# Token blocks of up to four units, alternating input places, and a mix in 32-column products

## The chip, the cores and the metric

The kernel runs on one core of one Trainium2 chip. The metric is the device time of one execution in microseconds; several runs are given by their median. A run of this kernel varies by some 0.2%.

## What is computed

Three layers follow each other. The first is a recurrent attention over 768 time steps for 4 x 8 heads of 48 channels; the second and the third are feed-forward layers of 3072 tokens x 384, one with 2048 hidden channels and a sigmoid gelu, the other with 1024 and a softmax-weighted, layer-normalised activation.

```python
def _attn_ref(r, k, v, w, u):
    for t in range(S):
        kt, vt, rt, wt = (k[:, :, t], v[:, :, t], r[:, :, t], w[:, :, t])
        cur = np.einsum('bhd,bhe->bhde', u[None] * kt, vt)
        y[:, :, t] = np.einsum('bhd,bhde->bhe', rt, state + cur)
        state = wt[:, :, :, None] * state + np.einsum('bhd,bhe->bhde', kt, vt)
def _moe_ref(x, w_in, w_out):
    h = x @ w_in
    return (h * (1.0 / (1.0 + np.exp(-1.702 * h)))) @ w_out
def _moe2_ref(x, w_in, w_out, g_ln):
    h = x @ w_in
    e = np.exp(h - np.max(h, axis=-1, keepdims=True))
    solu = h * e / (np.sum(e, axis=-1, keepdims=True) + 1e-09)
    mu = np.mean(solu, axis=-1, keepdims=True)
    var = np.mean((solu - mu) ** 2, axis=-1, keepdims=True)
    return ((solu - mu) / np.sqrt(var + 1e-06) * g_ln) @ w_out
```

The weights come as 64-bit floats; the kernel turns them into 32-bit ones on the chip.

## The kernel before

The 3072 tokens are 24 units of 128. A unit is 128 time steps of one batch entry, all eight heads; six units in a row carry a state. `BLOCKS` (line 28) groups the units for the first feed-forward layer: three blocks of two units and six of three. `LAST` is the last block's number.

**Attention of a unit.** `f_scan`, `f_r1`, `f_r0`, `f_back` and `f_k` (lines 133 to 165) form running products of the decay and scale `r` and `k` by them (VectorE, `f_r1` on GpSimd, a small copy `pc` on ScalarE). `turn_k` and `copy_k` transpose the scaled `k`. `scores` multiplies `k` by `r` within a half of 64 time steps, `masked` keeps the lower triangle and writes it into `R0` and `R1`, beside the scaled `r`. `states` and `update` carry the state. `mix` (line 308) is one product per head and half: `R0` or `R1` is the stationary operand, 64 columns of it, and `vs0` or `vs1`, state and values, the moving operand of 48 columns; the two halves write partitions 0 to 63 and 64 to 127 of one bank. `bonus`, `bonus_sum`, `bonus_mul` and `total` add the term with `u`. `turn` transposes the result; `out_hi` and `out_lo` split it into a high and a low part, `XH` and `XL`, which together keep 32-bit accuracy in products of the faster type. `XH` and `XL` have room for six units, used as a ring (line 383, 345).

**First feed-forward layer.** For a block and each of 16 slices `f` of the hidden channels: `rise` (line 517) makes nine products into a bank `h` (two banks by turns), `gelu` runs twice on ScalarE, `rest` forms the low part on VectorE, `fall` (line 541) makes nine products into three sums `acc`. `fall` runs two steps after `rise` (`drain(2)`). At a block's end `store` copies the sums to `x2a` or `x2b`, where the second layer reads them. A product has as many moving columns as the block has tokens: 256 or 384.

**Order.** Everything is put in order by hand. `START` (line 38) is a list of steps for the opening: attention of units 0 to 8, the conversion of the first layer's weights (`Lw` load, `N0` to `N3`, `H`, `C`), and the blocks 0 to 2. The raw weights pass through three places in `x2b` (`raw1`), the temporaries through six in `x2a` (`temp1`), since both are free then. From block 3 on, `steps_of` (line 654) hangs the attention of the next block's units between the 16 steps of a block, at the steps `ones` and `twos` and the ones behind them: `one`, `scan`, `back`, `two`, `rest_of`. During the last block the weights of the second layer are converted in the same way (`w2_steps`).

**Tail.** For each unit: `head` (line 580, 18 products of 512 columns), `soft` on ScalarE and VectorE, `turn_q` (transposes and split, into the room of `XH` and `XL`), `tail` (24 products of 384 columns), store.

Of the kernel before, what the change touches and what calls it, by code (L numbers as in the profile page):

```python
# [9 lines left out]
U32 = mybir.dt.uint32  # L10
# [16 lines left out]

BLOCKS = [(0, 2), (2, 2), (4, 2)] + [(u, 3) for u in range(6, NU, 3)]
LAST = len(BLOCKS) - 1

PASSED = (0, 1, 2, 4, 5, 6, 8, 9, 10, 12, 13, 15, 16, 17, 17, 17)
# [39 lines left out]
class Attention:  # L71
# [236 lines left out]
    def mix(self, i, e=None):  # L308
        mm, s = self.nc.tensor.matmul, self.st[i]
        one = e is None  # L310
        if i < QUADS:
            s["y"] = y = self.bank(i, 1)[:, 0:HD]
            y = [y[:, h * D:(h + 1) * D] for h in range(H)]
        else:

            s["y"] = y = self.bank(i, 3).rearrange("p (b c) -> p b c", b=2)[:, :, 4 * C:4 * C + 4 * D]
            y = [y[:, h // 4, (h % 4) * D:(h % 4 + 1) * D] for h in range(H)]
        if e is not None:
            mm(out=s["y"], lhsT=self.ident, rhs=s["vd"], start=True, stop=False)
        for h in range(H):  # L320
            c, e = slice(h * C, (h + 1) * C), slice(h * D, (h + 1) * D)
            mm(out=y[h][0:64], lhsT=s["R0"][0:112, c], rhs=s["vs0"][0:112, e], start=one, stop=one or h == 7)  # L322
            mm(out=y[h][64:128], lhsT=s["R1"][:, c], rhs=s["vs1"][:, e], start=one, stop=one or h == 7)  # L323

# [18 lines left out]

    def out_hi(self, i, hi):
        s, t = self.st[i], slice((i % 6) * 128, (i % 6) * 128 + 128)
        s["xv"] = s["xT"][:, 0:HD].rearrange("p (c t) -> p c t", c=3)
        self.nc.scalar.activation(out=hi[:, :, t], in_=s["xv"], func=AF.Copy)

    def out_lo(self, i, hi, lo, e=None):
        s = self.st.pop(i)  # L350
        t, x = slice((i % 6) * 128, (i % 6) * 128 + 128), s["xv"]
        if e is None:
# [10 lines left out]
def rwkv_moe_moe2(ctx: ExitStack, tc: tile.TileContext, rkw, nat, vn, v2n, cst, w1, w2i, w2o, gln, out):  # L363
# [10 lines left out]
    x2a = cp.tile([128, 4 * 1152], F32, name="x2a")  # L374
    x2b = cp.tile([128, 4 * 1152], F32, name="x2b")

    x2 = {}
    for b, (u0, n) in enumerate(BLOCKS):
        if b < 2:
            u0, n = 0, 4  # L380
        t = (x2a, x2b)[u0 // 12][:, (u0 % 12) * HD:(u0 % 12 + n) * HD]
        x2[b] = u0, t.rearrange("p (c t) -> p c t", c=3)
    XH, XL = (cp.tile([128, 3, 6 * 128], F32R, name=f"xT{a}") for a in "hl")

# [16 lines left out]
    def gtile(a, name):  # L401
        return cp.tile([128, 384], F32R, tag=a, name=name, bufs=3)

# [17 lines left out]
    def raw1(f):  # L421
        return x2b[:, (f % 3) * 1536:(f % 3 + 1) * 1536].bitcast(U32)

# [5 lines left out]

    order = START.split()  # L430
    def temp1(f):
        return x2a[:, (f % 6) * 768:(f % 6 + 1) * 768]

# [20 lines left out]
    def w2_steps(p):  # L454
# [8 lines left out]
        def load(src, n):  # L463
            raw = p.tile([128, 768], U32, tag="raw", name="raw", bufs=5)[:, 0:2 * n]
            t = p.tile([128, 384], U32, tag="t", name="t", bufs=7)[:, 0:n]
# [47 lines left out]
    def tokens(j):  # L513
        u0, n = BLOCKS[j]
        return n * 128, slice((u0 % 6) * 128, (u0 % 6 + n) * 128)

    def rise(j, f):
        TB, tok = tokens(j)
        h_ps = G[j, f] = single(f"h{j}_{f}")[:, 0:TB]
# [32 lines left out]

    def store(j, outs):
        for e in outs:
            nc.scalar.activation(out=x2[j][1][:, e], in_=acc[e][:, 0:512 if j < 2 else tokens(j)[0]], func=AF.Copy)
# [13 lines left out]

    XS, Q, O, SM, E = {}, {}, {}, {}, {}  # L570

# [49 lines left out]
    def turn_q(i, halves=(0, 1)):  # L621

        o = (i % 2) * 1024
        hi, lo = [t.rearrange("p c t -> p (c t)")[:, o:o + 1024] for t in (XH, XL)]
        for b in halves:
# [8 lines left out]
    def tail(i, part):  # L634
# [11 lines left out]
        o_ps = O.pop(i)  # L646
        ob = gtile("gh", f"ob{i}").bitcast(F32)
        nc.scalar.activation(out=ob, in_=o_ps, func=AF.Copy)
# [5 lines left out]
    def steps_of(j):  # L654
# [4 lines left out]
        u0, n = BLOCKS[j + 1]  # L659
        ones, twos = (1, 6, 11), (4, 9, 14)  # L660
        for i, a, b in zip(range(u0, u0 + n), ones, twos):
# [18 lines left out]

            def back(i=i, nx=nx, nn=nn):
                if nn:
                    at.f_back(i + 2)
                if nx:
                    at.bonus_sum(i + 1)

            def two(i=i, nx=nx):
                at.turn(i)
                if nx:
                    at.states(i + 1)  # L690
                    at.load_v2(i + 2)
                at.out_hi(i, XH)
                at.out_lo(i, XH, XL)
                if nx:
# [5 lines left out]

            def rest_of(i=i):
                at.f_r0(i + 2)
                at.f_k(i + 2)

            S[a] += [one]
            if nn:
                S[a + 1] += [scan]
            S[a + 2] += [back]
            S[b] += [two]
# [9 lines left out]
        D=at.states, DA=lambda i: at.states(i, 0), DB=lambda i: at.states(i, 1), U1=lambda i, e=None: at.update(i, 0, e), U2=lambda i, e=None: at.update(i, 1, e), X=at.mix, V=at.total,  # L719
        T=at.turn, O=lambda i: at.out_hi(i, XH), OL=lambda i, e=None: at.out_lo(i, XH, XL, e),  # L720
        N0=lambda f: conv1(f, 0), N1=lambda f: conv1(f, 1), N2=lambda f: conv1(f, 2), N3=lambda f: conv1(f, 3),
# [156 lines left out]
```

## Time and profile before

| what | value |
|---|---|
| median of 3 runs | 754.5 us (753.58 to 754.74) |
| the profiled execution, its own time | 753.76 us |
| its span, first to last instruction | 750.8 us |
| TensorE products, busy | 732.8 us (98%) |
| TensorE weight loads, busy | 688.8 us |
| VectorE busy | 502.2 us (67%) |
| ScalarE busy | 304.0 us (40%) |
| GpSimd busy | 153.3 us (20%) |
| mean granted TensorE clock | 0.999 of full speed |

Busy times of TensorE come from products that overlap each other in the pipeline, so the sum of their durations is larger than the time that they take in a row. The start-to-start distance of two products is what one costs in a full stream. All rows are of one profiled execution. Names: PE is TensorE, PEld its weight loads, DVE VectorE, ACT ScalarE, POOL GpSimd, SP the queue that issues the transfers.

### The profile page before, as it was taken

The numbers are of one execution on the slowest core, as the hardware profiler recorded it, in microseconds if no ns is written. First come the engines' busy times: TensorE is split into PE (matmuls) and PEld (weight loads), VectorE is DVE, ScalarE is ACT, GpSimd is POOL, SyncE is SP. The second block draws the span as 40 slices with busy tenths as digits, with TensorE's granted clock in tenths as the row PEclk, the third lists the DMA queues.
The fourth block names the chain that finished last, engine by engine and source line by source line (L and its number), as shares of the span: only waits on it lengthen the run. The fifth ranks groups of instructions, "written<-read, shape, count | busy, mean of one in ns | idle before, by whom it ended". The sixth has DMA issues, their size and how long they took to land.

```text
span 750.8 us, 15429 instructions
## 1 busy us (share of the span) xinstructions
PE 732.8 (98%) x6350; PEld 688.8 (92%) x6350; DVE 502.2 (67%) x885; ACT 304.0 (40%) x660; POOL 153.3 (20%) x158
## 2 busy tenths in 40 slices
PE   3899999999999999999999999999999999999998
PEld 2689999999999999999999999999999999999987
DVE  8899999887666665666566552498555555555553
ACT  2465453333223223322322322475544444444443
POOL 5351312541222222222222120040000000000000
PEclk9999999999999999999999999999999999999999
DMA  8965723334222221222222100451000000000000
GB/s 254 237 221 176 243 76 116 97 86 113 75 74 69 73 71 41 74 75 74 66 75 65 32 6 2 134 153 51 1 22 22 21 22 22 22 22 22 31 23 32
DMA packets 26103, 58.02 MB, mean 77 GB/s; under 512 B 3409, under 2 KB 18769, under 8 KB 26033
## 3 DMA queue, kind: packets, MB, share of 16 engines
q1 hardware_dynamic: 26032, 57.04, 25.7%
q8 instruction: 49, 0.80, 0.5%
q14 instruction: 22, 0.17, 0.1%
HBM read 52.31 MB, written 4.72 MB: 76 GB/s over the span
## 4 chain that ended last, share of the span: by engine, by line
PE 96%; DVE 2%; ACT 1%; issue 0%; DMA 0%; ACTq 0%; DVEq 0%
PE acc L548 28%; PE h L523 27%; PE o L641 13%; PE left L588 7%; PE right L588 7%; PE att L322 3%; PE right L628 1%; PE left L628 1%; PE att L215 1%; PE att L238 1%; PE att L338 1%; PE att L263 1%; PE d L446 1%; PE att L231 0%; PE att L275 0%
## 5 line engine op out<-in xcount | busy, mean ns | idle before, releaser
L548 PE MATMUL acc<-gh,w 128*128 128x384 f32 (+1 forms) x864 | 224.0, 323 | 0.0
L523 PE MATMUL h<-xTh,w 128*128 128x384 f32 (+1 forms) x864 | 180.2, 319 | 0.0
L531 ACT ACTIVATE gh<-h 128x384 fp32r<-128x384 f32 (+1 forms) x144 | 65.6, 455 | 266.4 <-PE h L523 257.9
L548 PEld LDWEIGHTS acc<-gh,w 128*128 128x128 f32 x864 | 152.7, 189 | 2.3
L538 DVE TENSOR_TENSOR gl<-h,gh 128x384 fp32r<-128x384 f32 (+1 forms) x144 | 73.4, 511 | 121.4 <-ACT h L533 120.9
L523 PEld LDWEIGHTS h<-xTh,w 128*128 128x128 f32 x864 | 142.9, 189 | 1.0 <-ACT w L448 0.5
L548 PE MATMUL acc<-gl,w 128*128 128x384 f32 (+1 forms) x432 | 137.3, 318 | 0.1
L523 PE MATMUL h<-xTl,w 128*128 128x384 f32 (+1 forms) x432 | 90.6, 318 | 0.0
L548 PEld LDWEIGHTS acc<-gl,w 128*128 128x128 f32 x432 | 81.7, 189 | 0.3 <-DVE gl L538 0.3
L523 PEld LDWEIGHTS h<-xTl,w 128*128 128x128 f32 x432 | 72.0, 189 | 0.0
L142 POOL TENSOR_TENSOR R<-rkw,P 64x512 f32<-64x512 f32 x24 | 30.5, 1272 | 197.2 <-DVE P L136 182.2
L641 PE MATMUL o<-w,xTh 128*128 128x384 f32 x384 | 70.5, 335 | 0.0
L641 PEld LDWEIGHTS o<-w,xTh 128*128 128x128 f32 x384 | 67.0, 188 | 0.2
L533 ACT ACTIVATE h<-h 128x384 f32<-128x384 f32 (+1 forms) x144 | 65.1, 452 | 0.0
L203 POOL TENSOR_TENSOR vd<-vs,dg 64x384 f32<-64x384 f32 x48 | 43.7, 910 | 78.7 <-PE att L338 55.6
L618 POOL TENSOR_TENSOR sm<-sm,mhalf 128x1 f32<-128x1 f32 x24 | 13.2, 548 | 218.5 <-DVE sm L617 218.5
L250 DVE TENSOR_TENSOR R<-att,cc 64x256 f32<-64x256 f32 (+1 forms) x82 | 37.2, 454 | 10.9 <-PE att L323 9.5
L641 PE MATMUL o<-w,xTl 128*128 128x384 f32 x192 | 43.0, 346 | 0.0
L613 ACT ACTIVATE e<-q,sm 128x1024 f32<-128x1024 f32 x24 | 27.6, 1152 | 30.3 <-DVE sm L616 29.8
L588 PE MATMUL right<-w,x2h 128*128 128x512 f32 x144 | 37.1, 392 | 0.0
L588 PE MATMUL left<-w,x2h 128*128 128x512 f32 x144 | 37.0, 392 | 0.0
L179 POOL TENSOR_TENSOR nr<-nr,nk 128x384 f32<-128x384 f32 x24 | 26.0, 1083 | 43.5 <-DMA nk<-in_nat 42.4
(170 smaller groups left out, 1255.6 us busy)
## 6 DMA issues: line engine op xcount, KB each, us to landing
rkw<-in_rkw SPq DMA_DIRECT2D x22, 676.4 KB, 5.3
x2b<-in_w SPq DMA_DIRECT2D x16, 768.0 KB, 5.0
nr<-in_nat SPq DMA_DIRECT2D x24, 192.0 KB, 3.0
nk<-in_nat SPq DMA_DIRECT2D x24, 192.0 KB, 2.6
vs<-in_vn SPq DMA_DIRECT2D x48, 96.0 KB, 4.4
out<-ob SPq DMA_DIRECT2D x24, 192.0 KB, 1.9
raw<-in_w2o SPq DMA_DIRECT2D x8, 384.0 KB, 3.3
v<-in_v2n SPq DMA_DIRECT2D x24, 96.0 KB, 2.5
```

The costliest lines, as they stand in the source:

```text
L142: (e or self.nc.gpsimd).tensor_tensor(out=heads(R1[0:64]), in0=heads(s["rkw"][0:64, 0:HC]), in1=heads(s["P"])[0:64, :, 0:C], op=ALU.mult)
L179: g.tensor_tensor(out=s["nr"], in0=s["nr"], in1=s["nk"], op=ALU.mult)
L203: nc.gpsimd.tensor_tensor(out=heads(vd[q:q + 64]), in0=heads(vt[q:q + 64]), in1=dg[q:q + 64].unsqueeze(2).to_broadcast([64, H, D]), op=ALU ...
L250: self.nc.vector.tensor_tensor(out=heads(R[q:q + 64])[:, h:h + n], in0=a, in1=m.unsqueeze(1).to_broadcast([64, n, C]), op=ALU.mult)
L523: nc.tensor.matmul(out=h_ps, lhsT=W1[f][:, ws + c * 128:ws + (c + 1) * 128], rhs=xs[:, c, tok], start=n == 0, stop=n == 8)
L531: nc.scalar.activation(out=gh, in_=h_ps, func=AF.Gelu_apprx_sigmoid)
L533: return nc.scalar.activation(out=h_ps, in_=h_ps, func=AF.Gelu_apprx_sigmoid)
L538: nc.vector.tensor_tensor(out=gl_, in0=g, in1=gh.bitcast(F32), op=ALU.subtract)
L548: nc.tensor.matmul(out=a, lhsT=W1[f][:, ws + e * 128:ws + (e + 1) * 128], rhs=gs, start=first and n == 0, stop=last and n == 2)
L588: nc.tensor.matmul(out=h_ps[:, b * 512:(b + 1) * 512], lhsT=xs[:, c], rhs=W2I[c][wb][:, b * 512:(b + 1) * 512], start=n == 0 and c == 0, s ...
L613: nc.scalar.activation(out=e, in_=q, func=AF.Square, bias=sm[:, 3:4], accum_out=sm[:, 4:5])
L641: nc.tensor.matmul(out=O[i], lhsT=(lo if n == 2 else hi)[:, f * 128:(f + 1) * 128], rhs=W2O[f][n == 1], start=n == 0 and f == 0, stop=n == ...
```

## The change

- `BLOCKS` becomes 2, 2, 2, 3, 3, 4, 4, 4 units: eight blocks for nine. The products of the last three have 512 moving columns. `steps_of` spreads four units over 16 steps, one every four steps, in the block before each of these.
- The inputs of the first layer get two places of four units each, used by turns (`PLACE`, `X`), for the ring of six units.
- `x2b` is smaller, and the last block's sums go to the room of one input place (`x2c`). The third raw buffer of the conversion goes to `x2a`, two temporaries to the room of the last weight slice. The quotients' split in the tail goes to the room of weight slices 12 to 15. `w2_steps` has four raw buffers for five.
- `mix` makes each product of 64 stationary columns as two of 32, with explicit tile positions.
- In `steps_of`, `bonus_sum` is a step of its own, at other places; `rest_of` does `f_k` first. In blocks of four `back` shares the step of `scan`.

```diff
-BLOCKS = [(0, 2), (2, 2), (4, 2)] + [(u, 3) for u in range(6, NU, 3)]
+BLOCKS = [(0, 2), (2, 2), (4, 2), (6, 3), (9, 3), (12, 4), (16, 4), (20, 4)]
+PLACE = {u + k: (0, 2 + k) if j == 1 else ((j + 1) % 2 if j > 1 else 0, k) for j, (u, n) in enumerate(BLOCKS) for k in range(n)}
...
         for h in range(H):
-            c, e = slice(h * C, (h + 1) * C), slice(h * D, (h + 1) * D)
-            mm(out=y[h][0:64], lhsT=s["R0"][0:112, c], rhs=s["vs0"][0:112, e], start=one, stop=one or h == 7)
-            mm(out=y[h][64:128], lhsT=s["R1"][:, c], rhs=s["vs1"][:, e], start=one, stop=one or h == 7)
+            e = slice(h * D, (h + 1) * D)
+            for t in (0, 32):
+                w = slice(h * C + t, h * C + t + 32)
+                mm(out=y[h][t:t + 32], lhsT=s["R0"][0:112, w], rhs=s["vs0"][0:112, e], start=one, stop=one or h == 7, tile_position=(0, t))
+                mm(out=y[h][64 + t:96 + t], lhsT=s["R1"][:, w], rhs=s["vs1"][:, e], start=one, stop=one or h == 7, tile_position=(0, 64 + t))
...
-    def out_hi(self, i, hi):
-        s, t = self.st[i], slice((i % 6) * 128, (i % 6) * 128 + 128)
+    def out_hi(self, i, X):
+        s, (g, t) = self.st[i], PLACE[i]
+        hi, t = X[g][0], slice(t * 128, t * 128 + 128)
...
-    x2b = cp.tile([128, 4 * 1152], F32, name="x2b")
+    x2b = cp.tile([128, 4 * 768], F32, name="x2b")
...
-    XH, XL = (cp.tile([128, 3, 6 * 128], F32R, name=f"xT{a}") for a in "hl")
+    X = [[cp.tile([128, 3, 512], F32R, tag="x2c" if g and a == "l" else f"xT{a}{g}", name=f"xT{a}{g}", bufs=1) for a in "hl"] for g in range(2)]
...
     def raw1(f):
-        return x2b[:, (f % 3) * 1536:(f % 3 + 1) * 1536].bitcast(U32)
+        t, k = (x2a, 2) if f % 3 == 2 else (x2b, f % 3)
+        return t[:, k * 1536:(k + 1) * 1536].bitcast(U32)
...
     def temp1(f):
-        return x2a[:, (f % 6) * 768:(f % 6 + 1) * 768]
+        if f % 6 < 4:
+            return x2a[:, (f % 6) * 768:(f % 6 + 1) * 768]
+        if not WF:
+            WF.append(wp.tile([128, 1536], F32, tag=f"w{NF1 - 1}", name="wf"))
+        return WF[0][:, (f % 6 - 4) * 768:(f % 6 - 3) * 768]
...
-            raw = p.tile([128, 768], U32, tag="raw", name="raw", bufs=5)[:, 0:2 * n]
+            raw = p.tile([128, 768], U32, tag="raw", name="raw", bufs=4)[:, 0:2 * n]
...
     def store(j, outs):
+        if j == LAST and j not in x2:
+            t = cp.tile([128, 1536], F32, tag="x2c", name="x2c", bufs=1)
+            x2[j] = BLOCKS[j][0], t.rearrange("p (c t) -> p c t", c=3)
...
     def turn_q(i, halves=(0, 1)):
-        o = (i % 2) * 1024
-        hi, lo = [t.rearrange("p c t -> p (c t)")[:, o:o + 1024] for t in (XH, XL)]
+        for a in "hl":
+            if (i % 2, a) not in QT:
+                QT[i % 2, a] = wp.tile([128, 1536], F32R, tag=f"w{12 + len(QT)}", name=f"q{a}{i}")
+        hi, lo = (QT[i % 2, a][:, 0:1024] for a in "hl")
...
-        ones, twos = (1, 6, 11), (4, 9, 14)
+        ones, twos = ((0, 4, 8, 12), (2, 6, 10, 14)) if n == 4 else ((1, 6, 11), (4, 9, 14))
...
-            def back(i=i, nx=nx, nn=nn):
-                if nn:
-                    at.f_back(i + 2)
-                if nx:
-                    at.bonus_sum(i + 1)
+            def back(i=i):
+                at.f_back(i + 2)
+            def sums(i=i):
+                at.bonus_sum(i + 1)
...
             def rest_of(i=i):
+                at.f_k(i + 2)
                 at.f_r0(i + 2)
-                at.f_k(i + 2)
...
-            S[a + 2] += [back]
+            if nx:
+                S[a if n == 4 else b - 1] += [sums]
+            if nn:
+                S[a + (1 if n == 4 else 2)] += [back]
```

## Rows read from the trace of the kernel before

**Rows 1.** Page: busy time; shares of the last-ending chain by line

```profile
PE 732.8 (98%) x6350; PEld 688.8 (92%) x6350; DVE 502.2 (67%) x885; ACT 304.0 (40%) x660; POOL 153.3 (20%) x158
PE acc L548 28%; PE h L523 27%; PE o L641 13%; PE left L588 7%; PE right L588 7%; PE att L322 3%; PE right L628 1%; PE left L628 1%; PE att L215 1%; PE att L238 1%; PE att L338 1%; PE att L263 1%; PE d L446 1%; PE att L231 0%; PE att L275 0%
```

**Rows 2.** Stretches: length, then busy us of PE, PEld, DVE, ACT, POOL

```profile
63.80:176.00 112.20, 112.03 (x1357) 109.26 (x1356) 101.63 (x168) 49.59 (x125) 37.04 (x32) 1.00 0.41 128
248.90:309.20 60.30, 60.30 (x599) 58.12 (x598) 38.39 (x65) 18.20 (x44) 15.20 (x15) 1.00 0.26 70
536.00:751.00 215.00, 211.42 (x1159) 193.44 (x1157) 120.86 (x253) 99.67 (x184) 12.60 (x23) 1.00 0.06 23
```

**Rows 3.** PE waits, 0 to 60 us: line, releaser, total, times, longest

```profile
PE att L231 <- DVE rkw L164: 8.5, 1, 8.5
PE att L338 <- ACT vd L332: 0.7, 1, 0.7
```

**Rows 4.** Chain in order of time: start, length, line, number of products

```profile
63.94 2.16 PE h L523 x18
526.46 4.68 PE acc L548 x27
```

**Rows 5.** Timeline of PE, one head: start, length, line, count

```profile
548.81 1.55 PE L588 MATMUL left<-w,x2h 128*128 128x512 f32 x6
550.89 1.52 PE L588 MATMUL left<-w,x2h 128*128 128x512 f32 x6
552.93 0.27 PE L628 MATMUL right<-cc,q 128*128 128x128 f32 x1
```

**Rows 6.** Timeline of PE, one mix

```profile
300.21 0.26 PE L322 MATMUL att<-vs,R 112*64 112x48 f32 x1
300.31 0.22 PE L323 MATMUL att<-vs,R 128*64 128x48 f32 x1
...
301.13 0.22 PE L323 MATMUL att<-vs,R 128*64 128x48 f32 x1
```

**Rows 7.** Timeline of PE, one states step and the product before it

```profile
170.40 0.28 PE L548 MATMUL acc<-gh,w 128*128 128x256 f32 x1
170.76 0.21 PE L263 MATMUL att<-vs,kTs 64*48 64x48 f32 x1
...
170.86 0.21 PE L266 MATMUL att<-v,kTs 64*48 64x48 f32 x1
...
171.13 0.20 PE L266 MATMUL att<-v,kTs 64*48 64x48 f32 x1
```

**Rows 8.** Timeline of PE, full 32-bit products with 384 columns

```profile
27.73 0.81 PE L446 MATMUL d<-x2a,cc 128*128 128x384 f32 x2
28.08 0.64 PE L447 MATMUL d<-w,neg 128*128 128x384 f32 x1
```

**Rows 9.** Waits of PE's weight loads in one attention block

```profile
PEld att L215 <- DVE rkw L164: 0.5, 2, 0.2
```

**Rows 10.** Timeline of PE around one turn_k

```profile
378.23 0.34 PE L523 MATMUL h<-xTh,w 128*128 128x384 f32 x1
378.49 0.60 PE L215 MATMUL att<-cc,rkw 112*128 112x112 f32 x4
```

**Rows 11.** DVE groups, one attention block: count, busy us, mean ns

```profile
L538 DVE TENSOR_TENSOR gl<-h,gh 128x384 fp32r<-128x384 f32 x17 | 9.5, 558 | 20.5 <-ACT h L533 20.5
L148 DVE TENSOR_TENSOR R<-rkw,P 48x512 f32<-48x512 f32 x3 | 2.1, 689 | 0.1
```

**Rows 12.** Timeline of DVE, f_r0 beside the f_r1 of GpSimd

```profile
167.51 1.41 DVE L148 TENSOR_TENSOR R<-rkw,P 48x512 f32<-48x512 f32 x1
```

**Rows 13.** Page: transfers, count, size, median us to landing

```profile
x2b<-in_w SPq DMA_DIRECT2D x16, 768.0 KB, 5.0
```

**Rows 14.** Groups of ACT: store by width

```profile
L555 ACT ACTIVATE x2b<-acc 128x384 f32<-128x384 f32 x12 | 5.1, 490 | 5.3 <-PE acc L548 5.3
L555 ACT ACTIVATE x2a<-acc 128x512 f32<-128x512 f32 x3 | 1.6, 597 | 0.4 <-PE acc L548 0.4
```

More of the change, by code (lines that the diff above doesn't have):

```diff
@@ L342, in out, with out_lo @@
         self.nc.scalar.activation(out=x[:, :, i * 128:(i + 1) * 128], in_=xT, func=AF.Copy)
-    def out_hi(self, i, hi):
-        s, t = self.st[i], slice((i % 6) * 128, (i % 6) * 128 + 128)
+    def out_hi(self, i, X):
+        s, (g, t) = self.st[i], PLACE[i]
+        hi, t = X[g][0], slice(t * 128, t * 128 + 128)
         s["xv"] = s["xT"][:, 0:HD].rearrange("p (c t) -> p c t", c=3)
         self.nc.scalar.activation(out=hi[:, :, t], in_=s["xv"], func=AF.Copy)
-    def out_lo(self, i, hi, lo, e=None):
-        s = self.st.pop(i)
-        t, x = slice((i % 6) * 128, (i % 6) * 128 + 128), s["xv"]
+    def out_lo(self, i, X, e=None):
+        s, (g, t) = self.st.pop(i), PLACE[i]
+        (hi, lo), t, x = X[g], slice(t * 128, t * 128 + 128), s["xv"]
         if e is None:
@@ L380, in rwkv_moe_moe2 @@
             u0, n = 0, 4
-        t = (x2a, x2b)[u0 // 12][:, (u0 % 12) * HD:(u0 % 12 + n) * HD]
-        x2[b] = u0, t.rearrange("p (c t) -> p c t", c=3)
-    XH, XL = (cp.tile([128, 3, 6 * 128], F32R, name=f"xT{a}") for a in "hl")
+        if b < LAST:
+            t = (x2a, x2b)[u0 // 12][:, (u0 % 12) * HD:(u0 % 12 + n) * HD]
+            x2[b] = u0, t.rearrange("p (c t) -> p c t", c=3)
+    X = [[cp.tile([128, 3, 512], F32R, tag="x2c" if g and a == "l" else f"xT{a}{g}", name=f"xT{a}{g}", bufs=1) for a in "hl"] for g in range(2)]
     def banks(name, side, shapes):
@@ L401, in gtile @@
     def gtile(a, name):
-        return cp.tile([128, 384], F32R, tag=a, name=name, bufs=3)
+        return cp.tile([128, 512], F32R, tag=a, name=name, bufs=3)
     def narrow(raw, t, steps=(0, 1, 2, 3)):
@@ L430, in rwkv_moe_moe2 @@
     order = START.split()
+    WF = []
     def temp1(f):
-        return x2a[:, (f % 6) * 768:(f % 6 + 1) * 768]
+        if f % 6 < 4:
[3 more added lines that the diff above has]
+        return WF[0][:, (f % 6 - 4) * 768:(f % 6 - 3) * 768]
     def conv1(f, k):
@@ L514, in tokens @@
         u0, n = BLOCKS[j]
-        return n * 128, slice((u0 % 6) * 128, (u0 % 6 + n) * 128)
+        g, k = PLACE[u0]
+        return n * 128, X[g], slice(k * 128, (k + n) * 128)
     def rise(j, f):
-        TB, tok = tokens(j)
+        TB, (XH, XL), tok = tokens(j)
         h_ps = G[j, f] = single(f"h{j}_{f}")[:, 0:TB]
@@ L567, in drain @@
             fall(j, f, f == 0, f == NF1 - 1)
-    XS, Q, O, SM, E = {}, {}, {}, {}, {}
+    XS, Q, O, SM, E, QT = {}, {}, {}, {}, {}, {}
     def xsplit(i):
@@ L646, in tail @@
         o_ps = O.pop(i)
-        ob = gtile("gh", f"ob{i}").bitcast(F32)
+        ob = gtile("gh", f"ob{i}")[:, 0:HD].bitcast(F32)
         nc.scalar.activation(out=ob, in_=o_ps, func=AF.Copy)
@@ L691, in two @@
                     at.load_v2(i + 2)
-                at.out_hi(i, XH)
-                at.out_lo(i, XH, XL)
+                at.out_hi(i, X)
+                at.out_lo(i, X)
                 if nx:
@@ L719, in rwkv_moe_moe2 @@
         D=at.states, DA=lambda i: at.states(i, 0), DB=lambda i: at.states(i, 1), U1=lambda i, e=None: at.update(i, 0, e), U2=lambda i, e=None: at.update(i, 1, e), X=at.mix, V=at.total,
-        T=at.turn, O=lambda i: at.out_hi(i, XH), OL=lambda i, e=None: at.out_lo(i, XH, XL, e),
+        T=at.turn, O=lambda i: at.out_hi(i, X), OL=lambda i, e=None: at.out_lo(i, X, e),
         N0=lambda f: conv1(f, 0), N1=lambda f: conv1(f, 1), N2=lambda f: conv1(f, 2), N3=lambda f: conv1(f, 3),
```

## The prediction, made before the changed kernel was run

> **What bounds the kernel now.** I read the engine totals and the chain of waits first, to see which engine sets the end: TensorE is busy for 98% of the span, and lines 548, 523, 641 and 588, all TensorE products, make up most of the chain [rows 1]. Busy time counts overlapped products, so I then asked stage by stage. In the table of stretches [rows 2] TensorE fills 112.03 of 112.20 us of the opening from 63.8 us on, all 60.30 us of one attention block and 211.4 of 215.0 us of the tail. VectorE, the next engine, has 38.4 of 60.3 us in the attention block. The listed waits of TensorE lie in the first 60 us; the largest is 8.5 us for the first `kt` [rows 3], and it is there before any changed line runs. After that the kernel is a row of products without holes. So a change is worth what it takes out of the TensorE stream, plus or minus the holes that it makes.
>
> **Part 1: twelve units in blocks of four.** Units 12 to 23 now take four blocks of three units; after, three blocks of four. A block always has 288 big products (16 steps of 9 in `rise` and 9 in `fall`), with 128 columns per unit. I need the start-to-start distance by width. At 256 columns 18 products take 2.16 us, 0.120 us each; at 384 columns 27 take 4.68 us, 0.1733 us each [rows 4]. The step of 128 columns is 0.0533 us, and about 0.013 us comes on top of it each time. So 512 columns should take 0.1733 + 0.0533 = 0.2266 us. The trace has this width only in `head` (line 588): the second nine take 552.93 - 550.89 = 2.04 us, 0.2267 each, the first nine 2.08 us, 0.2311 each [rows 5]. I take 0.2267, since `rise` and `fall` show no such irregular half, and keep 0.2311 as the bound. Before: 4 x 288 x 0.1733 = 199.6 us. After: 3 x 288 x 0.2267 = 195.9 us. **Gain 3.7 us** (at the bound 3 x 288 x 0.2311 = 199.7, so none). The elementwise work is the same per token, with fewer instructions.
>
> **Part 2: the mix in products of 32 columns.** One mix has 32 hardware products (16 calls, and the trace has two records for each). They start in 16 pairs, an `R0` product and an `R1` product each, from 300.21 to 301.13 us; the 14 distances from the second pair on take 0.82 us, 0.0586 each [rows 6]. After, each pair becomes four products of 32 weight columns, 64 in all, still 16 groups. What sets the 0.0586? Four tiles of 48 weight columns and 48 moving columns (`states`) run their 32 products from 170.76 to 171.13 us in eight groups; the last six distances take 0.27 us, 0.045 each [rows 7]. The moving side of the mix is also 48 columns, so I read its 64 weight columns as what separates 0.0586 from 0.045. With 32 columns that bound goes away and the moving side is left. A group of four then takes 0.040 to 0.045 us: 384 moving columns of a product of this type start the next one after at most 0.35 us [rows 8], 0.91 ns a column, 0.044 us for 48. I take 0.045, the row that it is nearest to. Saved: 16 x (0.0586 - 0.045) = 0.22 us per unit, 24 units, **5.2 us**; at 0.040 it is 7.1 us. All 24 count: after 63.8 us TensorE is full, and in the first 60 us `total` (line 332) waits for the mix, so it lies on the chain there too. Nothing in the trace has four column tiles on the same rows, so the upper bound is open; two values for it stand under the rivals.
>
> **A rule against this.** In the rows just named 32 products of four tiles, each with its own weight load, start 0.0116 us apart [rows 7], right after a hole of 0.36 us in the stream, so a store of products built up behind long ones doesn't explain it all. The Trainium skill, "TensorEngine Tiling", Instruction Overhead, says that a matmul has about 60 cycles of overhead and that no tiling factor is to be taken from a dimension that is already small. By an estimate from that page, with 60 cycles of 2.4 GHz, 64 x 25 ns would make a mix of 1.6 us. The trace disagrees for these four tiles, though they lie on two row groups and the new ones on one.
>
> **Part 3: the order of steps.** `rest_of` now does `f_k` before `f_r0`. `turn_k` waits for `f_k` in two of three units of a block [rows 9]; the first transpose then starts 0.26 us after the last product [rows 10], where a big product takes 0.173 [rows 4]. `f_k` is ready 0.69 us earlier, the time of `f_r0` [rows 11], so about 0.08 us less goes in some nine units, **0.7 us**. `scores` needs `f_r0` about 0.5 us after `turn_k`, so that is still in time. In blocks of four, `back` comes right behind `scan`, so ScalarE's small copy `pc` waits for the scan with the next gelu behind it, and `bonus_sum` stands right behind `total`, where it waits for GpSimd's `bonus`, issued two steps (over 6 us) before. The cover is the two-step lag of `fall` and the second `h` bank. VectorE's load is highest where four units' attention falls into a block of three units (12 to 15 during 9 to 11): 38.4 us less 17 x 0.558 is 28.9 us for three units [rows 2, 11], 9.6 each; 4 x 9.6 + 16 x 0.56 = 47.5 us in about 63 us, 75%. The second scan now also runs beside GpSimd's `f_r1`; a VectorE operation beside that one took 1.41 instead of 0.69 us [rows 11, 12], so up to 0.7 us more per unit, 80%. I put **0.2 us** on this and keep 2 us (half a microsecond in each of four units) as the bound.
>
> **Part 4: places.** The conversion still has three raw buffers and six temporaries, in other tiles; the weight loads take 5.0 us to land [rows 13] and no TensorE wait lies behind them in rows 2. Cost nothing; if the cover were gone, one load late costs up to 5.0 us. The temporary in the place of `w15` is read last by `C:11`, long before `H:15`. Four raw buffers for `w2` instead of five: those loads are half as large and are asked for two or more steps of about 4 us ahead; nothing. The two places of inputs: each is written one block after its last read; no wait. The quotients' split goes to `w12` to `w15`, free two steps before; nothing. The last `store` copies 512 columns instead of 384 with the next `head` behind it, 0.60 against 0.49 us [rows 14]: +0.1 us.
>
> **The sum**, against the profiled execution of 753.76 us (span 750.8): -3.7 - 5.2 - 0.7 + 0.2 + 0.1 = -9.3, so 744.5. The median of the runs is 0.74 us higher; forecast **745.2 us**. A measurement tells about 0.2%, 1.5 us, from no change.
>
> **Rivals.**
> - *A, the forecast* (743 to 747.5), 0.62.
> - *B, the mix keeps its rhythm* of 0.0586 us a group, because something other than the weight columns sets it. For it: only two widths are to be compared, 64 and 48. Against it: the moving side is the same in both and the times differ. 754.5 less the other parts, 3.7 + 0.7 - 0.3 = 4.1, is 750.4. Chance 0.10. That is also the case that this part doesn't do what it says.
> - *C, the four tiles don't run side by side.* The four read all rows at once: 192 moving columns per group. In the trace no stretch reads more than about 2.26 columns per ns on a row (512 in 0.2267 us [rows 5]; `states` two tiles' 96 in 0.045 [rows 7]). Were that a limit, a group takes 192 / 2.26 = 85 ns, the mix 16 x 0.0264 = 0.42 us more, 24 units 10.1 us: 754.5 - 4.1 + 10.1 = **760.5**. It turns the sign where a group takes over 58.6 + 4100 / 384 = 69 ns. For it: nothing shows four. Against it: two tiles' columns do run at once without loss. Chance 0.13.
> - *D, VectorE's order bites*: gelu or `gl` late in the dense block, 2 to 3 us: about 748. Chance 0.10. For it: the waits that Part 3 puts in a row. Against it: 75 to 80% load, and the lag of two steps.
> - *E, each product keeps its present distance* in the mix, 0.92 / 31 = 0.030 us [rows 6]: 64 take 1.9 us, 24 x 0.97 = 23 us more, 754.5 - 4.1 + 23 = 773. Chance 0.03. Against it: the products of [rows 7] start 0.0116 us apart. The rule of the Trainium skill's "TensorEngine Tiling" named above would act in this way.
> - What is left, 0.02: an unseen wait that makes it slower.
>
> **How the numbers follow.** The likeliest case gives 745.2. A, B and D hold 0.82: from 742.5 (A with a group of 0.040 us is 16 x 0.005 x 24 = 1.9 us less, 743.3; without the 0.3 us of waits and copies 743.0) to 751, past B. Faster by over 0.2% means under 753.0: A, B and D, 0.82; within 0.2% is the part of C with a group near 70 ns, 0.03; slower is the rest of C, E and what is left, 0.15.
>
> **What would show it.** Line 322 and 323 products at 64 per unit, the last starting about 0.70 us after the first (0.92: B; 1.3: C; 1.9: E). Lines 523 and 548 at 512 columns in nine per 2.04 us. `turn_k` no longer waiting for line 164. Still no VectorE, ScalarE or DMA among TensorE's waits after 60 us; a row of line 538 or 155 there would be D. Wrong I'd be, above all, if four column tiles share what two have now.

## The result and the profile after

| | before | after |
|---|---|---|
| median of 4 runs each | 754.04 us (752.66 to 754.74) | 742.62 us (742.21 to 743.39) |
| the profiled execution | 753.76 us | 743.39 us |
| its span | 750.8 us | 741.6 us |
| from the first product of block 3 to the end | 575.96 us | 567.25 us |

The ratio is 0.9852, with a 95% interval of 0.9835 to 0.9869. The changed kernel is 11.4 us faster by the medians; the forecast was 745.2, 2.6 us more than what came. The lines have moved: `mix` is 327 and 328 now, `rise` 540, `fall` 565, `store` 575, `head` 608, `f_k` 166, `turn_k` 217.

The page of after, busy time, and the last-ending chain by line (the counterpart of [rows 1]):

```profile
PE 722.6 (97%) x6830; PEld 645.9 (87%) x6830; DVE 508.9 (69%) x869; ACT 299.9 (40%) x625; POOL 161.4 (22%) x158
PE acc L565 28%; PE h L540 27%; PE o L663 13%; PE left L608 7%; PE right L608 7%; PE att L327 2%; PE right L650 1%; PE left L650 1%; PE att L217 1%; PE att L240 1%; PE att L343 1%; PE att L265 1%; PE att L328 1%; PE d L462 1%; DVE P L138 0%
```

The bound has not changed: the chain is still TensorE's products. There are 480 records more of them (24 mixes of 64 for 32, less the products that the merge saves), and yet 10 us less of busy time. The stretches of after, columns as in [rows 2]: the block of three in which four units' attention falls, the first block of four, and all from block 3 on.

```profile
232.62:295.23 62.61, 62.42 (x829) 60.06 (x829) 50.09 (x81) 19.34 (x47) 24.56 (x20) 1.00 0.32 87
295.23:372.25 77.02, 77.02 (x829) 63.71 (x829) 54.88 (x81) 22.77 (x47) 24.16 (x21) 1.00 0.28 76
...
174.37:741.62 567.25, 563.64 (x4617) 500.92 (x4615) 352.31 (x626) 223.20 (x447) 99.00 (x100) 1.00 0.18 51
```

The block of four is full, 77.02 of 77.02 us. The dense block has 0.19 us of holes, and VectorE is busy for 50.09 of its 62.61 us, 80%. TensorE's waits from block 3 up to the first `head` (174 to 530 us) tell the same, those of its products first and then those of its weight loads, each in the columns of [rows 3]:

```profile
PE acc L565 <- ACT x2a L575: 0.2, 1, 0.2
```

```profile
PEld att L265 <- issue: 2.3, 14, 0.2
PEld att L327 <- issue: 0.4, 1, 0.4
PEld acc L565 <- ACT x2a L575: 0.3, 1, 0.3
PEld left L608 <- ACT x2c L575: 0.2, 1, 0.2
```

The row of `turn_k` waiting for `f_k`, the counterpart of [rows 9], is gone. The two rows that name ScalarE's store are small: once a `fall` waits 0.3 us for the store of the block ahead of it, and the first `head` 0.2 us for the last store. The forecast's signs had no row of ScalarE. The second row is in before too, ahead of its own first `head` at 531.06 us; the first is new, and the section on the prediction comes back to it.

The timeline of TensorE at one mix of after, counterpart of [rows 6] (the first two groups of four, the last, and the product behind it):

```profile
197.88 0.23 PE L327 MATMUL att<-vs,R 112*32 112x48 f32 x1
197.88 0.23 PE L328 MATMUL att<-vs,R 128*32 128x48 f32 x1
197.89 0.23 PE L327 MATMUL att<-vs,R 112*32 112x48 f32 x1
197.90 0.23 PE L328 MATMUL att<-vs,R 128*32 128x48 f32 x1
197.94 0.21 PE L327 MATMUL att<-vs,R 112*32 112x48 f32 x1
...
198.54 0.21 PE L327 MATMUL att<-vs,R 112*32 112x48 f32 x1
...
198.56 0.21 PE L328 MATMUL att<-vs,R 128*32 128x48 f32 x1
198.70 0.44 PE L565 MATMUL acc<-gh,w 128*128 128x384 f32 x1
```

Four products start within some 0.02 us and then comes the next group; 14 distances from the second group to the last take 198.54 - 197.94 = 0.60 us, 0.043 each. Last start less first is 0.68 us, where it was 0.92. The four tiles do run side by side, and the group is shorter than the forecast's 0.045.

The timeline at a `rise` of 512 columns, between two `fall` (the counterpart of [rows 5]):

```profile
358.95 0.84 PE L540 MATMUL h<-xTh,w 128*128 128x512 f32 x3
...
360.99 0.39 PE L565 MATMUL acc<-gh,w 128*128 128x512 f32 x1
```

Nine products take 360.99 - 358.95 = 2.04 us, 0.2267 each: the value that Part 1 took.

### The profile page after: what moved, and what is told of

The parts are those of the page before. It is cut to its first block, busy times and chain, and to the rows that moved or that the text cites. A ratio compares the mean times of both kernels' runs of the same rounds, so it can differ in the third digit from the quotient of the medians.

```text
span 741.6 us, 16318 instructions
## 1 busy us (share of the span) xinstructions
PE 722.6 (97%) x6830; PEld 645.9 (87%) x6830; DVE 508.9 (69%) x869; ACT 299.9 (40%) x625; POOL 161.4 (22%) x158
## 4 chain that ended last, share of the span: by engine, by line
PE 96%; DVE 2%; ACT 1%; issue 1%; DMA 0%; ACTq 0%; DVEq 0%
PE acc L565 28%; PE h L540 27%; PE o L663 13%; PE left L608 7%; PE right L608 7%; PE att L327 2%; PE right L650 1%; PE left L650 1%; PE att L217 1%; PE att L240 1%; PE att L343 1%; PE att L265 1%; PE att L328 1%; PE d L462 1%; DVE P L138 0%
## 5 line engine op out<-in xcount | busy, mean ns | idle before, releaser
L565 PE MATMUL acc<-gh,w 128*128 128x256 f32 (+2 forms) x768 | 212.3, 342 | 0.2 <-ACT x2a L575 0.2
L540 PE MATMUL h<-xTh,w 128*128 128x256 f32 (+2 forms) x768 | 173.8, 337 | 0.0
L548 ACT ACTIVATE gh<-h 128x256 fp32r<-128x256 f32 (+2 forms) x128 | 63.0, 492 | 253.2 <-PE h L540 245.0
L555 DVE TENSOR_TENSOR gl<-h,gh 128x256 fp32r<-128x256 f32 (+2 forms) x128 | 70.6, 553 | 105.0 <-ACT h L550 104.4
L565 PE MATMUL acc<-gl,w 128*128 128x256 f32 (+2 forms) x384 | 129.0, 336 | 0.0
L540 PE MATMUL h<-xTl,w 128*128 128x256 f32 (+2 forms) x384 | 87.4, 336 | 0.0
L663 PE MATMUL o<-w,qh 128*128 128x384 f32 x384 | 70.5, 334 | 0.0
L663 PEld LDWEIGHTS o<-w,qh 128*128 128x128 f32 x384 | 67.0, 188 | 0.2
L550 ACT ACTIVATE h<-h 128x256 f32<-128x256 f32 (+2 forms) x128 | 62.4, 488 | 0.0
L663 PE MATMUL o<-w,ql 128*128 128x384 f32 x192 | 43.0, 346 | 0.0
```

Source lines behind the costliest of these rows:

```text
L540: nc.tensor.matmul(out=h_ps, lhsT=W1[f][:, ws + c * 128:ws + (c + 1) * 128], rhs=xs[:, c, tok], start=n == 0, stop=n == 8)
L548: nc.scalar.activation(out=gh, in_=h_ps, func=AF.Gelu_apprx_sigmoid)
L550: return nc.scalar.activation(out=h_ps, in_=h_ps, func=AF.Gelu_apprx_sigmoid)
L555: nc.vector.tensor_tensor(out=gl_, in0=g, in1=gh.bitcast(F32), op=ALU.subtract)
L565: nc.tensor.matmul(out=a, lhsT=W1[f][:, ws + e * 128:ws + (e + 1) * 128], rhs=gs, start=first and n == 0, stop=last and n == 2)
L663: nc.tensor.matmul(out=O[i], lhsT=(lo if n == 2 else hi)[:, f * 128:(f + 1) * 128], rhs=W2O[f][n == 1], start=n == 0 and f == 0, stop=n == ...
```

## Experiments

The theory: all of the gain is work taken out of the TensorE stream, by the mix, the merge and the order of the steps, and these add up. The rivals: the gain of one part comes from another (VectorE's order, say), the parts depend on each other, or the mix is faster for a reason other than its stationary columns. Where only one execution of a kernel is at hand, or where less than 1 us matters, I compare the stretch from the first product of block 3 to the end: it was 575.96 and 576.09 us in two executions of before and 567.25 and 567.26 in two of after, while the opening ahead of it scatters by some 2 us. The first four kernels shared their runs of before (median 753.54 of 9).

**The mix undone.** The changed kernel with the mix in products of 64 columns:

```diff
-            for t in (0, 32):
-                w = slice(h * C + t, h * C + t + 32)
-                mm(out=y[h][t:t + 32], lhsT=s["R0"][0:112, w], ...
...
+            mm(out=y[h][0:64], lhsT=s["R0"][0:112, c], rhs=s["vs0"][0:112, e], ...
+            mm(out=y[h][64:128], lhsT=s["R1"][:, c], rhs=s["vs1"][:, e], ...
```

> The changed kernel with the mix back in products of 64 columns; blocks, places and order stay. Theory (the mix is worth what its groups save on TensorE): the groups of the changed kernel start 0.0425 us apart, those of before 0.0586, 16 groups, 24 units: 6.2 us slower than the changed kernel, about 748.8 us, and the groups are 0.0586 us apart again. Rival (a good part of the gain is in the blocks and places, the mix's saving is filled by other waits): 2 to 4 us slower, 744.6 to 746.6 us, with waits of TensorE that the changed kernel doesn't have being absent here.

Measured: 748.17 us (748.05 to 750.09), ratio to before 0.9938 [0.9924, 0.9953], 5.5 us over the changed kernel. Its stretches, the dense block and the first block of four:

```profile
234.27:297.85 63.58, 63.39 (x701) 61.08 (x701) 50.09 (x81) 19.33 (x47) 24.56 (x20) 1.00 0.31 85
297.85:375.90 78.05, 78.05 (x701) 64.78 (x701) 54.88 (x81) 22.77 (x47) 24.17 (x21) 1.00 0.27 75
```

With four mixes in each, the stretches grow by 0.97 and 1.03 us against after: 0.24 to 0.26 us a mix. VectorE's busy time is the same to 0.01 us. From block 3 on the span is 3.74 us longer, 0.25 for each of the 15 mixes there. The mix is worth what its own rhythm says, 16 x (0.0586 - 0.043) = 0.25.

**The mix alone.** The edit of the mix from the change, in the kernel before and with nothing else:

> The kernel before with the mix in products of 32 columns and nothing else of the change. Theory: 6.2 us faster than before, about 747.8 us, groups 0.0425 us apart, and turn_k still waits for line 164. Rival (the short mix needs the new order or the new places to pay): less than 4 us faster, with VectorE or ScalarE in TensorE's waits in the attention blocks.

Measured: 748.33 us (747.27 to 749.02), 0.9933 [0.9918, 0.9948]. The block of units 12 to 14, which takes 60.29 us in before:

```profile
291.74:351.30 59.56, 59.56 (x695) 57.35 (x694) 37.54 (x64) 18.21 (x44) 15.21 (x15) 1.00 0.25 71
```

It has three mixes and is 0.73 us shorter, 0.24 each. So the part gives the same without the rest of the change as with it. `turn_k` still waits for `f_k` 9 times there, 2.1 us in all of the weight loads' waits.

**The merge undone.** The changed kernel with units 12 to 23 in blocks of three again:

```diff
-BLOCKS = [(0, 2), (2, 2), (4, 2), (6, 3), (9, 3), (12, 4), (16, 4), (20, 4)]
+BLOCKS = [(0, 2), (2, 2), (4, 2), (6, 3), (9, 3), (12, 3), (15, 3), (18, 3), (21, 3)]
...
-    x2b = cp.tile([128, 4 * 768], F32, name="x2b")
+    x2b = cp.tile([128, 9 * 384], F32, name="x2b")
...
-        return cp.tile([128, 512], F32R, tag=a, name=name, bufs=3)
+        return cp.tile([128, 384], F32R, tag=a, name=name, bufs=3)
...
-            x2[j] = BLOCKS[j][0], t.rearrange("p (c t) -> p c t", c=3)
+            x2[j] = BLOCKS[j][0], t[:, 0:1152].rearrange("p (c t) -> p c t", c=3)
```

> The changed kernel with units 12 to 23 in blocks of three again; the mix, the two input places, the conversion's places and the order of steps stay. Theory (288 products per block, 0.1733 us at 384 columns and 0.2267 us at 512): 3.7 us slower than the changed kernel, about 746.3 us. Rival (products of 512 columns cost 0.2311 us as in the first nine of a head): no difference, 742.6 us. Rival (the new places bring time of their own): it stays more than 7.5 us faster than before, since mix 6.2 and order 0.7 make only 6.9.

Measured: 747.0 us (746.12 to 747.9), 0.9914 [0.99, 0.9929]; that is 4.4 us over the changed kernel by the medians, and 571.19 - 567.25 = 3.94 us from block 3 on. The same block as above:

```profile
291.87:351.17 59.30, 59.30 (x694) 57.48 (x694) 37.30 (x64) 18.20 (x44) 15.21 (x15) 1.00 0.26 71
```

This kernel has the mix and the order of the steps, and the new places. Its block is 0.99 us shorter than before's: 0.73 for the mix (above), 0.25 for the order (below), 0.01 left. The places cost nothing here.

**The order alone.** The kernel before with `f_k` ahead of `f_r0` in `rest_of`:

```diff
             def rest_of(i=i):
+                at.f_k(i + 2)
                 at.f_r0(i + 2)
-                at.f_k(i + 2)
```

> The kernel before with f_k ahead of f_r0 in rest_of and nothing else of the change. Theory: no wait of turn_k for line 164 in the attention blocks, the first transpose always 0.18 us after the last product, 0.7 us shorter between the start of the first and of the last block of three. Rival (the wait goes over to the scores, which need f_r0): the same length, with a wait of line 238 or 239 for line 148.

Measured: one execution, 752.76 us beside 755.77 of before in the same series; such a pair alone says little. The stretch of the same block, and the weight loads' waits from 234 to 473 us:

```profile
295.15:355.19 60.04, 60.04 (x599) 58.26 (x598) 37.24 (x64) 18.20 (x44) 15.19 (x15) 1.00 0.26 70
```

```profile
PEld att L263 <- issue: 1.8, 11, 0.2
PEld att L322 <- issue: 0.2, 1, 0.2
```

Before has a third row there, which is gone here:

```profile
PEld att L215 <- DVE rkw L164: 1.6, 7, 0.2
```

It is `turn_k` waiting for `f_k`. The block is 0.25 us shorter, and from block 3 to the end it is 751.0 - 176.11 = 574.9 us, 1.1 less than the 575.96 and 576.09 of before.

**The order undone.** The changed kernel with `f_r0` first:

```diff
             def rest_of(i=i):
-                at.f_k(i + 2)
                 at.f_r0(i + 2)
+                at.f_k(i + 2)
```

> The changed kernel with f_r0 ahead of f_k in rest_of again. Theory: in blocks of three units (9 to 11 attended, and 12 to 15 at four units in a block of three) turn_k waits for f_k again, about 0.08 us each, while in the blocks of four, with 4.1 us a step, it doesn't: together 0.2 to 0.5 us, below what a time can tell, but seen in TensorE's waits. Rival: no wait at all, then the order was not what removed it.

Measured: one execution of 743.56 us, 741.8 - 172.90 = 568.9 us from block 3 on, 1.65 more than after. The same two stretches as in after, and the weight loads' waits in the first of them:

```profile
231.41:295.36 63.95, 63.18 (x830) 59.78 (x830) 50.14 (x81) 19.40 (x47) 24.60 (x20) 1.00 0.32 85
295.36:372.38 77.02, 77.02 (x830) 63.66 (x829) 55.15 (x80) 22.76 (x47) 24.18 (x21) 1.00 0.28 76
```

```profile
PEld att L217 <- DVE rkw L166: 1.8, 4, 0.6
PEld att L265 <- issue: 0.7, 4, 0.2
PEld acc L565 <- ACT x2a L575: 0.3, 1, 0.3
```

The expectation was too small, and the place tells why. The block of four is the same, 77.02. The dense block is 1.34 us longer, with TensorE idle for 0.77 us, 0.58 more than in after, since each of its four `turn_k` waits for a VectorE that is 78% busy. The order matters most where VectorE has little to spare: block 3, the one ahead, is 0.26 us longer, the blocks of four not at all. With `f_k` later by one `f_r0`, 0.69 us [rows 11], the wait is as long as 0.6 us. In after's dense block `f_k` ends 0.16 to 0.63 us ahead of the first weight load of its `turn_k`, so it comes in time by little.

**What sets the rhythm of the mix.** Two kernels with half the moving columns in the mixes of units 12 to 23: only 24 of each head's 48 outputs are computed there, the other half is left out. First with 64 stationary columns, as in the mix undone, then with 32; the edit of the second:

```diff
+        n = D if i < 12 else 24
-                mm(out=y[h][t:t + 32], lhsT=..., rhs=s["vs0"][0:112, e], ...
+                mm(out=y[h][t:t + 32, 0:n], lhsT=..., rhs=s["vs0"][0:112, e][:, 0:n], ...
```

> The changed kernel with the mix in 64 columns and, for units 12 to 23, only 24 of the 48 moving columns of each product: half of each head's output is left out there. Theory (64 stationary columns set the distance of the groups): the groups of these units stay 0.0586 us apart, as with 48. Rival (the moving columns set it): they come down to about 0.03 us.

> The changed kernel with only 24 of the 48 moving columns in the products of the mix of units 12 to 23, in 32 stationary columns: half of each head's output is left out there. Theory (with 32 stationary columns the 48 moving ones set 0.0425 us): the groups come down, to 0.032 to 0.034 us. Rival (four products need 0.0425 us to be fed, 0.0106 each, whatever they hold): no difference, 0.0425 us.

Measured: one execution each, 746.92 and 742.2 us. The mix with 64 stationary and 24 moving columns:

```profile
236.14 0.22 PE L325 MATMUL att<-vs,R 112*64 112x24 f32 x1
...
236.90 0.22 PE L325 MATMUL att<-vs,R 112*64 112x24 f32 x1
```

From the third to the last group (13 distances) it takes 236.90 - 236.14 = 0.76 us, 0.0585 a group: the same as with 48 moving columns [rows 6]. Half of the moving columns changes nothing, so it isn't they that set it; what the changed mix cuts, the 64 stationary columns, does. The mix with 32 stationary and 24 moving columns:

```profile
235.72 0.19 PE L328 MATMUL att<-vs,R 112*32 112x24 f32 x1
...
235.94 0.19 PE L328 MATMUL att<-vs,R 112*32 112x24 f32 x1
...
236.04 0.19 PE L328 MATMUL att<-vs,R 112*32 112x24 f32 x2
236.06 0.19 PE L329 MATMUL att<-vs,R 128*32 128x24 f32 x2
```

Groups of four are 0.031 us apart up to 235.94 (seven distances in 235.94 - 235.72 = 0.22, 0.031 each), where they are 0.043 with 48 moving columns; so with 32 stationary columns the 48 moving ones set it. 0.031 is more than half of 0.043, and these rows don't tell what sets it there. From about 235.95 on a row of two products comes every 0.017 us, 8.4 ns a product, whatever the tile. A group of four would take 0.034 us at that pace, less than the 0.043 of after, so after's mix does not feel it.

**The same idea one step further.** The changed kernel with `scores`, which has 32 products of 64 stationary columns in four tiles, as 64 products of 32 columns in eight tiles:

```diff
-            mm(out=P[0:64, c], lhsT=kt[64:112, c], rhs=R0[64:112, c], ...
+            for t in (0, 32):
+                mm(out=P[t:t + 32, c], lhsT=kt[64:112, ct], rhs=R0[64:112, c], ..., tile_position=(64, t))
```

(and the other three products in the same way)

> The changed kernel with the scores of units 6 to 23 also in products of 32 stationary columns: eight tiles of 48 rows x 32 columns, 64 moving columns each, in place of four of 64. Theory (the moving columns set the group, 0.83 ns a column, and products of tiles can start faster than seen so far): a group goes from 0.0586 to about 0.056 us, 18 units, 0.4 us faster, about 742.2 us. Rival (a product needs some 0.0106 us of its own to start, a quarter of the new mix's 0.0425): eight take 0.085 us, a unit 0.2 us more, 18 units 3.8 us, about 746.4 us.

Measured: 744.81 us (744.15 to 745.6), 0.9886 [0.9871, 0.99]: 2.2 us slower than the changed kernel. One `scores` of this kernel:

```profile
297.51 0.22 PE L242 MATMUL att<-R,rkw 48*32 48x64 f32 x1
...
297.56 0.22 PE L242 MATMUL att<-R,rkw 48*32 48x64 f32 x1
...
297.67 0.22 PE L245 MATMUL att<-R,rkw 48*32 48x64 f32 x1
297.70 0.27 PE L242 MATMUL att<-R,rkw 48*32 48x64 f32 x2
...
298.07 0.22 PE L245 MATMUL att<-R,rkw 48*32 48x64 f32 x1
```

After the first group, the first 32 products come in groups of eight, 0.056 us apart. That is what the expectation took for 64 moving columns, but eight starts 7 ns apart make 0.056 us as well, so it doesn't tell the two apart. Then there are holes, and from 297.70 to 298.07 the other 32 need 0.37 us, 0.012 each on the mean: two every 0.017 us in the middle, one every 0.017 us at both ends. The whole has 0.64 us from first to last start, where the 32 wider ones of after have 0.48; 15 units x 0.16 is 2.4 us, about the loss that was measured. Both ideas were half right: a group of eight can take 0.056 us, but the products don't come that fast for long. Half as many columns with twice as many instructions gains only as long as the pace of the products is not the slower of the two.

**Before and after again,** for the stretch from block 3 on and for what lies outside the span.

> The kernel before once more, unchanged, for a second profiled execution: the first has 2.96 us of its time outside its span, the nine kernels profiled since have 1.75 to 1.80. Theory (that was this one execution): about 1.8 us outside, span 750 to 752 us, the first product of block 3 anywhere from 174 to 176 us. Rival (it belongs to the kernel, and the change or the new places take 1.2 us out of it): 2.9 us again.

> The changed kernel once more, unchanged, for a second profiled execution. Theory (the opening before block 3 scatters by about 1 us from one execution to the next, the rest doesn't): from the first product of block 3 to the end 567.2 us within 0.2, as before; the first product of block 3 somewhere from 172.9 to 174.8 us. Rival (the opening of this kernel is fixed at 174.4 us): 174.4 within 0.2.

Measured: 752.78 us with a span of 750.9, and 742.43 with 740.7. From block 3 on, first the kernel before:

```profile
174.77:750.86 576.09, 572.66 (x4425) 542.05 (x4423) 345.20 (x642) 227.34 (x482) 90.12 (x100) 1.00 0.18 51
```

and the changed one:

```profile
173.40:740.66 567.26, 563.64 (x4617) 500.94 (x4615) 352.38 (x626) 223.20 (x447) 99.01 (x100) 1.00 0.18 51
```

The difference is 8.8 us, where the first pair has 8.7. What lies outside the span is 1.9 us here for before, and 1.7 to 1.8 for after; in before's execution that the forecast started from it was 753.76 - 750.8 = 2.96. That is no property of the kernel before: most executions of all kernels have 1.7 to 2.1 us, and one of the mix alone has 748.94 - 746.0 = 2.94.

## Why the prediction was right, and where its terms were off

**Part 1, the merge**, foretold 3.7, measured 3.94 from block 3 on (4.4 by the medians, with the opening's scatter in it). With the distances unrounded (4.68 / 27 and 2.04 / 9) the forecast's own sum is 3.84. The width that only `head` showed [rows 5] carried over: 0.2267 us, not the bound of 0.2311.

**Part 2, the mix**, foretold 5.2: 0.22 in each of 24 units. Where the stream is full it gave more, 0.25, because the group is 0.043 us and not 0.045. In the opening the gain is harder to see. Block 3 starts at 173.76 us on the mean of seven executions of kernels with the new mix (172.90 to 174.74) and at 175.08 on the mean of five with the old one (174.35 to 176.11): 1.3 us earlier, where nine mixes at 0.25 are 2.25; but executions of one kind lie up to 1.8 us apart. Their traces tell more. From the first product of block 0 to that of block 3, with seven mixes, the five take 138.75 to 139.36 us and the seven 137.41 to 137.78: 1.5 us less on the mean, of 7 x 0.25 = 1.75. Each of these mixes has 0.68 us from first to last start, where the old one has 0.92. The scatter lies ahead of that, with the first product of block 0 anywhere from 35.1 to 37.3 us, and the first mix of all, at 24 us, gained nothing in after: from the start of the product ahead of it to that of the one behind it are 2.97 us there and 2.22 in before. So "all 24 count" was the weak sentence, by that mix above all; which wait keeps the small rest was not tried. In sum 3.74 + 1.3 = 5.0. The reading that the 64 stationary columns set the old rhythm was an inference from two widths; the half-width kernel and the changed mix bear it out.

**The rule against this** did not act. The Trainium skill, "TensorEngine Tiling", Instruction Overhead, gives some 60 cycles to a matmul; 64 products of a mix start within 0.68 us here, 10.6 ns each, and those of one group some 7 ns apart (in the timeline of after four start from 197.88 to 197.90). The trace disagrees for tiles that run beside each other, now for tiles on the same rows too.

**Part 3, the order**, foretold 0.7, measured 1.1 from block 3 on in the kernel before. Nine waits were foretold, and nine there are in before from block 3 on (2.1 us of the weight loads); the size was too small, 0.08 us each where 1.1 / 9 is 0.12. VectorE's load in the dense block was foretold as 75 to 80% and is 80%, and the second scan was foretold up to 0.7 us longer; it is 0.9. The group of that scan among VectorE's in the dense block, and then in the block ahead of it (columns as in [rows 11]):

```profile
L159 DVE TENSOR_TENSOR_SCAN rkw<-rkw,ipc 112x520 f32<-112x520 f32 x4 | 8.6, 2139 | 0.1
```

```profile
L159 DVE TENSOR_TENSOR_SCAN rkw<-rkw,ipc 112x520 f32<-112x520 f32 x3 | 3.7, 1242 | 0.1
```

ScalarE's `pc` does wait for the scan, as Part 3 feared (ScalarE's waits from 176 to 445 us):

```profile
ACT pc L157 <- DVE P L138: 18.5, 10, 1.9
```

Once it reaches TensorE, at the start of the dense block, by way of the store (after, ScalarE and then TensorE):

```profile
242.24 0.21 ACT L157 ACTIVATE pc<-P 112x8 f32<-112x8 f32 x1 [1.77 <-DVE P L138]
242.36 1.23 ACT L575 ACTIVATE x2a<-acc 128x384 f32<-128x384 f32 x3
```

```profile
243.65 0.45 PE L565 MATMUL acc<-gh,w 128*128 128x384 f32 x1 [0.19 <-ACT x2a L575]
```

The last products of block 3 start by 240.73 us, but the store of their sums stands behind `pc`, and the next `fall` behind the store. That is the new row of the waits above and the whole 0.19 us of holes in the dense block; the merge experiment, where `back` is one step later than `scan`, doesn't have it. So the 0.2 us put on these waits came, though by the store and not by a gelu or `gl`.

**Part 4, places.** No transfer is among TensorE's waits, and the block of three in the merge experiment leaves 0.01 us for them. The last store took 596 ns where 597 was taken. The first `head` waits 0.2 us for it, but so it does in before, with the narrower store:

```profile
PEld left L588 <- ACT x2b L555: 0.2, 1, 0.2
```

The wait is as long in both, so the +0.1 us did not come.

**The sum.** For the span it was 9.3 us, and 750.8 - 741.6 is 9.2. That this fits so well is partly luck. From block 3 on 7.4 us were foretold (15 x 0.22 + 3.7 + 0.7 - 0.3), and 8.7 came; the parts measured one by one, 3.74 + 3.94 + 1.1 = 8.8, make it up. Ahead of block 3 the forecast has 2.0 us (nine mixes), and this pair of executions shows 0.5, by the scatter and the first mix named above.

The 2.6 us by which the median lies under the forecast come from two other places. The profiled execution of before had 2.96 us outside its span, 1.1 more than most others (1.7 to 2.1), and the forecast kept that. And I added 0.74 because the median of before was above its profiled execution; the median of after is 0.77 below its own. 1.1 + 1.5 is 2.6. Both steps treat the one execution as typical; the span was the better base.

**The rivals.** The measured 742.6 us lies just under the range that A names, 743 to 747.5, for the two reasons above. B fell: the group is 0.043 us, not 0.0586. C fell too: four tiles on all rows read 192 moving columns per group in 0.043 us, 4.5 a nanosecond over the four tiles, twice what the old trace showed. E fell with the rule above. D came only in small, as the 0.19 us by way of the store. With `f_k` one operation later the dense block loses 1.34 us, still less than D's 2 to 3.

## What to carry to other kernels

When one engine's stream is full, price a change by the start-to-start distances in that stream: here the merge gave what its widths said to some tenths of a microsecond, and the mix 0.24 to 0.26 us wherever the stream was full. A change of order is worth what the waits of each block make of it: 0.25 us in a block of three of before, 1.34 in the dense block of after, nothing in the blocks of four. To make tiled products of small width faster, find which side sets the rhythm of a group (halve the moving columns and look whether it moves) and cut that side alone, as long as the products still come fast enough: the cut of the mix gained 5 us, the same cut of `scores` lost 2.2. Take the sum against the span, and look at how much of the one profiled time lies outside it and in a stretch that scatters.

## What the hardware showed that I had not expected

Small products come at two paces. A burst goes at 7 to 8 ns a product where the tiles allow it (0.031 us per group of four with 24 moving columns). After some 32 to 40 of them the pace falls: in the half-width mix to two products every 17 ns, 8.4 ns each, and in the split `scores`, between holes and single products, to the same two every 17 ns, 12 ns each on the mean. That the first ones were stored up while the array was at work on the large products ahead is my reading of it; no run tests that by itself.

The back scan of VectorE on 112 x 520 elements takes 1.24 us in one place and 2.14 in another, by the two groups above. In the second place GpSimd is at work during the whole of it, as its timeline and VectorE's show:

```profile
242.34 1.18 POOL L144 TENSOR_TENSOR R<-rkw,P 64x512 f32<-64x512 f32 x1 [10.77 <-issue]
243.49 1.76 POOL L205 TENSOR_TENSOR vd<-vs,dg 64x384 f32<-64x384 f32 x1
```

```profile
242.49 2.14 DVE L159 TENSOR_TENSOR_SCAN rkw<-rkw,ipc 112x520 f32<-112x520 f32 x1
```

The scan starts 0.15 us after `f_r1` (line 144), in all four units of that block; in the merge experiment the scans of these units have no GpSimd operation beside them and take 1.24 us. The traces also tell which of the two operations counts. The twelve executions have 576 scans of this size, the first and the back scan of each unit. Of these, 150 start while a GpSimd operation is under way, and a scan then takes 1.24 us plus what is left of that operation less some 0.14 us (plus nothing where no more than that is left): 1.50 us with 0.40 left, 1.92 with 0.82, 2.14 with 1.04. The 44 that start first, with a GpSimd operation starting during them, take 1.23 to 1.24 us, as the 382 with none beside them do. There GpSimd's operation is longer, where more than some 0.2 us of the scan is left: 2.07 us instead of 1.18 for an `f_r1` of the order undone, GpSimd and then VectorE:

```profile
5.26 2.07 POOL L144 TENSOR_TENSOR R<-rkw,P 64x512 f32<-64x512 f32 x1 [4.43 <-DMA rkw<-in_rkw]
```

```profile
5.12 1.24 DVE L159 TENSOR_TENSOR_SCAN rkw<-rkw,ipc 112x520 f32<-112x520 f32 x1
```

So in the dense block it is `f_r1`, under way when the scan starts, that costs VectorE 0.9 us in each of four units, 3.6 of its 50.09 us; line 205 costs the scan nothing. A kernel that starts the scan ahead of `f_r1` was not tried.
